# A recurrent-memory attention and a dilated local attention on one core: stage reports, output stores and a PSUM bank moved in the loop, working tiles and five weight units moved at its start

## The chip, the core and the metric

The kernel runs on one core of a Trainium2 chip. A core has a matrix engine (PE, with weight loads listed apart as PEld), a vector engine (DVE), a scalar engine (ACT), a general engine (POOL), an engine that only issues and synchronises (SP), and 16 DMA engines that all queues share. The metric is the device time of one execution in microseconds (us); the kernel is compared by the median of several runs.

## What is computed

The input `x` is 2048 rows of 640 numbers. Two branches are mixed by a gate per row:

```python
g = sigmoid((x * gate_w).sum(-1))
a = A_ref(x, mem0, Wq, Wk, Wv, Wo)      # branch A
b = B_ref(x, wqkv, wo)                  # branch B
return g * a + (1 - g) * b
```

Branch B is attention of 32 heads of width 20 over 8 earlier rows with a step of 2. Branch A is a recurrence over 64 segments of 32 rows. Its attention has 32 heads of width 192:

```python
for s in range(64):
    h = concat([mem, x[32*s:32*s+32]])         # 8 + 32 = 40 rows
    q, k, v = h @ Wq, h @ Wk, h @ Wv           # 640 -> 32 heads x 192
    p = softmax(masked(q @ k.T * 192**-0.5))
    o = (p @ v) @ Wo                           # 40 rows x 640
    mem = o[:8]
    outs.append(o[8:])
```

Each segment needs the memory that the one before left, so the segments run one after the other.

## The kernel before

The kernel has four parts in order of time. `part_b` computes branch B and writes its result, already weighted, to DRAM (`bsc_dram`), together with the transposed segments (`xh_dram`). `prepass` computes, for all segments at once, the projections of the eight last rows of each segment, and stores them to `zpk_dram`: first q and k (tiles `ZS`, pool `pre_zs`), then v (tiles `ZV`, pool `pre_zv`). `part_a` runs the recurrence. `part_z` finishes the eight last rows of every segment from `oz_dram`.

**Weights.** The weights of branch A do not all fit into SBUF. `weights_setup` splits them into units. Nine are loaded early, most of the others by `load_late(0)`, `load_late(1)` (in `prepass`, ahead of its v part) and `load_late(2)` (the last three units of `ob`, ahead of `part_a`). The 21 half units of the list `STREAM` are read from DRAM again in every segment, through a ring of seven slots (`wst`). `pump` issues the loads on SP's queue. A slot is loaded anew when PE has finished with the unit seven places back; the text numbers these units 0 to 20 in the order of `STREAM`.

**A segment.** `segment("head", ...)` projects q and k: `m_qk(0)` to `m_qk(3)` with units 0 to 5 of the stream, copies out of PSUM by `c_qk` on ACT, block transposes by `t_qk` on DVE. `segment("rest", ...)` does `m_qk(4)`, `m_qk(5)`, the scores in two halves, the softmax (`e_exp`, `e_sum`, `e_norm`), the v projection in three thirds (`m_v(0)` to `m_v(2)`, copied out by `c_v`), the product with the values (`pv_half`), and the output projection (`o_group`). At its end the memory rows go back into `hT` (`pick`), and the next head starts. `m_qk(i)` writes the PSUM banks `X[:,0]`, `X[:,1]`, `Ms[0]`, `Ms[1]`, `Ms[0]`, `X[:,1]` for i = 0 to 5.

**The loop.** The order of every engine's instructions in `part_a` is written out by hand (`manual_schedule`). The first segment and a head are unrolled; then `For_i` (line 1017) runs 62 passes, each a rest followed by the head of the next segment; a last rest follows. A pass is cut by `tc.stage_boundary()` into four stages: stage 0 from the start of the rest to `m_v(1,(0,))`, stage 1 to `o_group("oa", 3)`, stage 2 into the head behind `m_qk(0,(0,1,2))`, stage 3 to the end. Within a stage `done(engine)` (`tc.previous_stage_wait`) is a report of that engine: it waits until all that this engine issued in the previous stage, its DMAs included, has finished, and says so to the others. No engine enters the next stage before all five have reported in the present one; entering stage 0 of the next pass follows the same rule. Behind the entry, each engine resets semaphores and goes on. `held()` is SP's report followed by a halt of the pump until the next boundary. All these instructions carry line 1017 in the profile.

In a head of the loop the reports stand in this order: POOL, behind the two stores `store_z`; DVE behind `mix`; ACT behind `c_qk(1)`; SP and PE at the very end, behind `m_qk(3)`. SP's queue in the head holds the loads of units 6 to 12.

**Stores.** `store_z(s, h)` issues on POOL a DMA from `zst[h]` to `oz_dram[h]`. `zst[0]` is a part of `KW` (`aK` in the profile), which `c_qk(2)` of the next head overwrites; `zst[1]` is a part of `vz` (`aVz`), which `load_vz`, on POOL at the start of the rest, overwrites. In the loop both stores of segment s are issued in the next head, behind its stage boundary.

**The tiles of part A.** `part_a` allocates the working tiles (`aP`, `aK`, `aVz`, `aSel`, `aH`, `aG`), fills the selection masks (`build_sel`: small memsets on DVE, 40 or so selections on POOL), and loads the first segment into `aH`; then `load_z(0)` and `load_vz(0)` follow. All of it stands behind the release of the tiles of `prepass`.

Of the kernel before, what the change touches and what calls it, by code (L numbers as in the profile page):

```python
# [10 lines left out]
BF = mybir.dt.bfloat16  # L11
# [2 lines left out]

SLOTS = 7
N_EARLY = 9
LATE0 = 101376
STREAM = [("q", 0, 1, 1), ("k", 0, 1, 1), ("k", 0, 3, 1), ("q", 1, 1, 0), ("k", 1, 0, 0), ("k", 1, 3, 1), ("q", 2, 2,
          0), ("k", 2, 0, 1), ("k", 2, 1, 1), ("k", 2, 4, 1), ("v", 0, 3, 1), ("v", 1, 1, 0), ("v", 1, 4, 1), ("v", 2,
# [7 lines left out]
class _K:  # L27
# [381 lines left out]
    def weights_setup(self):  # L409
        nc, tc = self.nc, self.tc  # L410
        rest = [k for u in self.slice_keys() for k in self.parts(u) if k not in STREAM]
        first = ["q", "k", "v", "oa", "ob"]
        rest = sorted(rest, key=lambda k: first.index(k[0]))
        self.early, late = rest[:N_EARLY], rest[N_EARLY:]
        self.late = ([], [], late[-3:])
        used = 0
        for k in late[:-3]:
            used += 2 * self.width(k)
            self.late[int(used > LATE0)].append(k)
        self.wres = self.ctx.enter_context(tc.tile_pool(name="wres", bufs=1))  # L420
        self.res_tiles = {}
        self.wscr = {}
        self.wstream = self.ctx.enter_context(tc.tile_pool(name="wstream", bufs=1))
        self.slots = [self.wstream.tile([128, 1024], BF, name=f"wst{i}") for i in range(SLOTS)]
        self.slot_at, self.streaming = 0, False
# [77 lines left out]
    def prepass(self):  # L503

        nc, tc, KC = self.nc, self.tc, self.KC
        nseg = self.S // self.seg
        NZ = nseg * 8
        self.zpk_dram = self.dram.tile([nseg, 128, 1152], BF, name="zpk_dram")
        with tc.tile_pool(name="pre_zv", bufs=2, side="right", reuse_waits="tile") as zvp:
            zTi = zvp.tile([128, KC, NZ], BF, name="zTi", bufs=1)  # L510
            with tc.tile_pool(name="pre_zs", bufs=2, reuse_waits="tile") as zp, \
                    tc.tile_pool(name="pre_zt", bufs=1, reuse_waits="tile") as ztp:
                zT = ztp.tile([128, KC, NZ], BF, name="zT")
                nc.scalar.dma_start(zT[:], self.zT_dram[:].rearrange("p c s i -> p c (s i)"))
                nc.gpsimd.tensor_copy(zTi[:].rearrange("p c (i s) -> p c i s", i=8),
                                      zT[:].rearrange("p c (s i) -> p c i s", i=8))
                for m in ("q", "k"):
                    n = 16 if m == "q" else 24
                    for c in range(48):
                        if c % n == 0:  # L520
                            ZS = zp.tile([128, nseg, 192], BF, name="ZS")
                        if c % 16 == 0:
                            sls = [self.get_columns(m, c // 16, kc) for kc in range(KC)]
                        ps = self.pst([128, NZ], F32, name="ps_pre")
                        for kc in range(KC):
                            nc.tensor.matmul(ps[:], lhsT=sls[kc][c % 16],
                                             rhs=zT[:, kc, :], start=(kc == 0), stop=(kc == KC - 1))
                        zc = 8 * (c % 16) if m == "q" else 16 * (c % 12) + 8 * (c // 12 % 2)
                        self.evac(ZS[:, :, zc:zc + 8], ps[:].rearrange("p (s i) -> p s i", i=8))
                        if c % n == n - 1:  # L530
                            if m == "q":
                                zs = [(256 * (c // n) + 128, 0, 128)]
                            elif c < n:
                                zs = [(0, 0, 128), (256, 128, 64)]
                            else:
                                zs = [(320, 0, 64), (512, 64, 128)]
                            for z0, f, w in zs:
                                nc.scalar.dma_start(self.zpk_dram[:, :, z0:z0 + w].rearrange("s p f -> p s f"),
                                                    ZS[:, :, f:f + w])
            self.load_late(1)  # L540
            for t in range(3):
                sls = [self.v_columns(t, kc) for kc in range(KC)]
                for st in range(NZ // 128):
                    ZV = zvp.tile([128, 2048], BF, name="ZV")
                    pss = [self.pst([128, 512], F32, name="ps_pre") for _ in range(4)]
                    for kc in range(KC):
                        for j in range(4):
                            nc.tensor.matmul(pss[j][:], lhsT=zTi[:, kc, 128 * st:128 * st + 128],
                                             rhs=sls[kc][j], start=(kc == 0),
                                             stop=(kc == KC - 1))  # L550
                    for j in range(4):
                        self.evac(ZV[:, 512 * j:512 * j + 512], pss[j][:])
                    for k in range(2 * st, 2 * st + 2):
                        for e, R, x, n in self.V_PIECES[t]:
                            nc.scalar.dma_start(self.zpk_dram[:, 8 * R + k:128:32, 768 + x:768 + x + n],
                                                ZV[64 * (k % 2):64 * (k % 2) + 64, :].rearrange(
                                                    "s (j e) -> s j e", j=4)[:, :, e:e + n])

    def build_sel(self, W, ones):
        nc = self.nc  # L560
# [26 lines left out]
    def part_a(self):  # L587
# [2 lines left out]
        scale_a = float(self.Dh) ** (-0.5)  # L590
        ctx = ExitStack()
        with ctx:
            pers = ctx.enter_context(tc.tile_pool(name="a_pers", bufs=1))
            work = ctx.enter_context(tc.tile_pool(name="a_work", bufs=1))
            PP, KW, vz, sel, h_, a4 = (pers.tile([128, n], BF, name=x) for x, n in (
                ("aP", 2304), ("aK", 1024), ("aVz", 384), ("aSel", 188), ("aH", 160), ("aG", 162)))
            self.build_sel(sel, PP[:, 0:160])
            p0 = (128, 896, 1664)
            P = [PP[:, f:f + 640].rearrange("p (b c i) -> p b c i", b=5, i=8) for f in p0]
            Px = [PP[:, f + 128:f + 640] for f in p0]  # L600
# [33 lines left out]
            def row(t, s):  # L634
                return t[bass.ds(s, 1)].rearrange("o p f -> p (o f)")

            def load_seg(s, dst=xh):
                nc.sync.dma_start(dst, row(self.xh_dram, s))

            def load_z(s):  # L640
                nc.sync.dma_start(PP[:, 0:2304].rearrange("p (g f) -> p g f", g=3)[:, :, 0:256],
# [7 lines left out]

            def load_a4(s):  # L650
                nc.sync.dma_start(a4[:].bitcast(I32), self.bsc_dram[bass.ds(32 * s, 32)].rearrange("t j f -> j t f"))

            load_seg(0, h_[:])
            load_z(0)
            load_vz(0)

            def tail():
                pa = Ss[0][:, 0, :]
# [22 lines left out]
            def segment(part, prev, s, nxt, looped=False):  # L681
# [123 lines left out]

                def m_v(t, kcs=range(KC)):
                    if t not in pvs:
                        pvs[t] = Ms[1 - t % 2]
                    for kc in kcs:
                        sl = self.v_columns(t, kc)  # L810
                        burst([nc.tensor.matmul(pvs[t][32 * j:32 * j + 32, :], lhsT=hT[:, kc, :],  # L811
# [4 lines left out]

                def c_v(t):

                    (nc.vector.tensor_copy if t == 0 else nc.scalar.copy)(Px[t], pvs[t][:])  # L819

                def pv_half(h):
                    E = Es[h]
# [76 lines left out]
                if part == "head":  # L899
                    self.used = 0  # L900
                    m_qk(0, (0, 1, 2))
                    stage()
                    if prev is not None:
                        store_z(prev, 0)
                        store_z(prev, 1)
                    done(POOL)
                    m_qk(1, (0,))
                    if prev is not None:
                        pick("ob", Ss[1])
                    m_qk(1, (1, 2))  # L910
                    if prev is not None:
                        pa, ms = tail()
                        burst(ms)
                    m_qk(0, (3, 4)); m_qk(1, (3, 4))
                    if prev is not None:
                        mix(pa)
                    done(DVE)
                    c_qk(0); c_qk(1)
                    done(ACTE)
                    t_qk(0); t_qk(1)  # L920
                    m_qk(2, range(KC)); c_qk(2); t_qk(2)
                    m_qk(3, range(KC)); c_qk(3); t_qk(3)
                    done(SP)
                    done(PE)
                    return
                self.end = len(STREAM) if nxt is None else None
# [50 lines left out]
                for i2 in range(4):  # L977
                    o_group("oa", i2)
                stage()
                if nxt is None:  # L980
                    store_z(s, 0)
                done(POOL)
                pairs = pv_half(1)
                done(PE)
                c_o(1, pairs)
                c_z(1, pairs, 0); c_z(1, pairs, 1)
                done(ACTE)
                if nxt is None:
                    store_z(s, 1)
                if nxt is None:  # L990
                    self.sort_oz(0)
                for i2 in (4, 5):
# [17 lines left out]

            ctx.enter_context(tc.manual_schedule(engines=set(ALL)))
            self.start_stream()
            segment("head", None, 0, 1)
            segment("rest", None, 0, 1)
            self.sent -= len(STREAM)
# [69 lines left out]
def kernel(  # L1085
# [20 lines left out]
    with tc.tile_pool(name="psum", bufs=8, space=bass.MemoryType.PSUM) as k.psum:  # L1106
        with tc.issue_after(k.first_store):
            k.prepass()
    k.load_late(2)
    k.part_a()  # L1110

_INS = ['A_x', 'A_mem0', 'A_Wq', 'A_Wk', 'A_Wv', 'A_Wo', 'A_seg_len', 'B_x', 'B_wqkv', 'B_wo', 'gate_w']
# [29 lines left out]
```

## Time and profile before

| what | us |
|---|---|
| median of 3 runs (1679.66 to 1682.4) | 1680.38 |
| the profiled execution | 1679.99 |
| its span, first to last instruction | 1678.5 |
| branch B, to about | 229 |
| `prepass`, about | 229 to 428 |
| first matmul of `part_a` | 430 |
| one pass of the loop, mean (POOL's `load_vz`, 62 times from 462.6 to 1574.0) | 18.2 |
| `part_z` and the end, from about | 1606 |

The page of the profile gives the busy time of each engine. The waits view lists which engine waited for which, with the line of each: `PE psm L714 <- ACT aK L721` means that a matmul of line 714 writing PSUM tile `psm` waited for the ACT instruction of line 721 that writes `aK`. The timeline lists instructions in order, start and duration first; square brackets give the idle time of the engine before the instruction and what ended it. A "q" behind an engine's name is its sequencer: waiting, branching, issuing. The view of one source line gives counts, durations in ns (least, median, most), and the first and last start. The view of windows gives, for each stretch, its length, the busy time of PE, PEld, DVE, ACT and POOL, the granted clock of PE, the busy share of the DMA engines, and GB/s.

### The profile page before, as it was taken

What the parts mean: (1) busy time and instruction counts of PE and PEld (TensorE: products, weight loads), DVE (VectorE), ACT (ScalarE), POOL (GpSimd) and SP (SyncE); (2) the same over time, 40 slices, a digit from 0 to 9 for tenths busy, and PEclk for the clock granted to TensorE, in tenths of its full rate; (3) what the DMA queues carried; (4) which work ended last, traced back from release to release, by engine and by line L of the source; (5) the groups of instructions that cost most, each with busy time, mean ns of one, the idle gap of its engine ahead of it and who ended that gap; (6) DMA issues with size and microseconds to landing.
All of it is one profiled execution on the core that took longest, in us unless ns stands there. A gap on an engine that the chain in (4) does not pass through costs nothing. (4 is left out here: it accounts for less than half of the span.)

```text
span 1678.5 us, 91617 instructions
## 1 busy us (share of the span) xinstructions
PE 1486.7 (89%) x37462; PEld 852.0 (51%) x37477; DVE 802.7 (48%) x1936; ACT 656.1 (39%) x1609; POOL 143.2 (9%) x275
## 2 busy tenths in 40 slices
PE   6898897997689999999999999999999999999878
PEld 3455553343345555555555555555555555555457
DVE  4556542222345555555555555555555555555520
ACT  3766741212233433433433433443443343443340
POOL 4002000000200010010000001001001001001000
PEclk9999999999799999999999999999999999999989
DMA  6931059789679999999999999999999999999981
GB/s 165 215 101 53 31 157 266 181 204 290 213 247 317 307 316 318 301 305 320 307 300 318 314 301 311 314 306 317 315 303 312 316 305 310 317 310 310 316 209 28
DMA packets 438730, 438.32 MB, mean 261 GB/s; under 512 B 194172, under 2 KB 306820, under 8 KB 438660
## 3 DMA queue, kind: packets, MB, share of 16 engines
q1 hardware_dynamic: 344344, 395.02, 73.2%
q10 hardware_dynamic: 87148, 29.72, 7.2%
q0 software_dynamic: 7168, 12.60, 2.2%
q8 instruction: 51, 0.84, 0.2%
q14 instruction: 19, 0.16, 0.0%
HBM read 402.83 MB, written 39.48 MB: 264 GB/s over the span
## 5 line engine op out<-in xcount | busy, mean ns | idle before, releaser
L714 PEld LDWEIGHTS <-aH 128*32 128x32 bf16 x7680 | 201.2, 96 | 277.2 <-PE psm L714 79.6
L811 PE MATMUL psm<-wlate_v,aH 128*32 128x512 bf16 x3200 | 250.9, 382 | 18.1 <-DVE aP L819 16.7
L721 ACT CAST aP<-psx 128x512 bf16<-128x512 f32 x128 | 68.8, 589 | 327.9 <-PE psx L714 327.9
L714 PE MATMUL psx<-wlate_k,aH 128*32 128x512 bf16 x1920 | 195.6, 385 | 0.0
L874 PEld LDWEIGHTS <-aP 128*32 128x32 bf16 x6144 | 160.1, 96 | 64.1 <-ACT aP L853 23.1
L874 PE MATMUL psm<-wlate_oa,aP 128*32 128x384 bf16 x2560 | 167.7, 329 | 0.0
L714 PE MATMUL psm<-wlate_q,aH 128*32 128x512 bf16 x1408 | 108.8, 381 | 59.7 <-ACT aK L721 50.6
L734 DVE STREAM_TRANSPOSE aK<-aP 128x512 bf16<-128x512 bf16 (+1 forms) x256 | 142.6, 557 | 13.4 <-ACT aP L721 0.3
L714 PE MATMUL psx<-wst,aH 128*32 128x512 bf16 x768 | 138.8, 384 | 3.4 <-DMA wst<-wscr 3.4
L811 PEld LDWEIGHTS <-aH 128*32 128x32 bf16 x3840 | 94.5, 97 | 82.5 <-issue 20.0
L731 DVE STREAM_TRANSPOSE aP<-aP 128x512 bf16<-128x512 bf16 x128 | 91.1, 712 | 89.2 <-ACT aP L721 89.0
L874 PE MATMUL psm<-wst,aP 128*32 128x384 bf16 (+1 forms) x896 | 128.9, 306 | 4.7 <-DMA wst<-wscr 4.7
L874 PE MATMUL psm<-wlate_ob,aP 128*32 128x256 bf16 x2688 | 125.3, 273 | 0.4 <-issue 0.4
L811 PE MATMUL psm<-wst,aH 128*32 128x512 bf16 x640 | 124.7, 383 | 0.0
L714 PE MATMUL psx<-wres_q,aH 128*32 128x512 bf16 x1152 | 97.4, 385 | 19.1 <-DMA aH<-xh_dram 14.6
L853 DVE CAST aP<-psx 128x128 bf16<-128x128 f32 (+2 forms) x192 | 75.6, 422 | 70.5 <-PE psx L841 70.4
L773 ACT ACTIVATE aK<-psS 128x224 bf16<-128x224 f32 x128 | 46.1, 360 | 148.8 <-PE psS L765 148.8
L774 DVE TENSOR_TENSOR aK<-aK,aSel 128x224 bf16<-128x224 bf16 x128 | 35.3, 275 | 139.1 <-ACT aK L773 138.6
L714 PE MATMUL psm<-wst,aH 128*32 128x512 bf16 x512 | 99.6, 380 | 0.9 <-DMA wst<-wscr 0.6
L853 ACT CAST aP<-psS 128x384 bf16<-128x384 f32 (+2 forms) x192 | 65.4, 375 | 83.5 <-PE psx L841 81.6
L648 POOL DMA_DIRECT2D oz_dram<-aK x64 | 34.6, 541 | 734.8 <-DMA aVz<-zpk_dram 712.9
L819 ACT CAST aP<-psm 128x512 bf16<-128x512 f32 x128 | 75.4, 589 | 47.3 <-PE psS L765 45.0
(164 smaller groups left out, 2750.5 us busy)
## 6 DMA issues: line engine op xcount, KB each, us to landing
wst<-wscr SPq DMA_DIRECT2D x965, 256.0 KB, 4.4
wst<-wscr SPq DMA_DIRECT2D x384, 192.0 KB, 3.5
aP<-zpk_dram SPq DMA_DIRECT2D x64, 192.0 KB, 3.1
zpk_dram<-ZS ACTq DMA_DIRECT2D x5, 2048.0 KB
aVz<-zpk_dram POOLq DMA_DIRECT2D x64, 96.0 KB, 4.0
wlate_k<-in_A_Wk_dram SPq DMA_DIRECT2D x8, 512.0 KB
wres_q<-in_A_Wq_dram SPq DMA_DIRECT2D x7, 512.0 KB
wst<-in_A_Wk_dram SPq DMA_DIRECT2D x14, 256.0 KB
```

What stands on the lines that cost most here:

```text
L648: nc.gpsimd.dma_start(row(self.oz_dram[h], s), zst[h])
L714: burst([nc.tensor.matmul(pq[32 * j:32 * j + 32, :], lhsT=hT[:, kc, :], rhs=sl[j], start=(kc == 0), stop=(kc == KC - 1), tile_position=(0, ...
L721: nc.scalar.copy(st[i], pqs[i])
L731: nc.vector.transpose(P[p][:, 1:5, :, :].rearrange("p b c i -> p c b i"), st[i])
L734: nc.vector.transpose(KT[:, c0:c1, :].rearrange("p c k -> p (c k)"), st[i] if part is None else st5[part])
L773: nc.scalar.activation(E, pSs[h][:, :, 0:112], ACT.Exp, scale=scale_a)
L774: nc.vector.tensor_tensor(out=E, in0=E, in1=self.mask[h].unsqueeze(1).to_broadcast([128, 2, 112]), op=ALU.mult)
L811: burst([nc.tensor.matmul(pvs[t][32 * j:32 * j + 32, :], lhsT=hT[:, kc, :], rhs=sl[j], start=(kc == 0), stop=(kc == KC - 1), tile_position ...
L819: (nc.vector.tensor_copy if t == 0 else nc.scalar.copy)(Px[t], pvs[t][:])
L853: (nc.scalar.copy, nc.vector.tensor_copy)[g](x.rearrange("p (j c q) -> p j c q", j=2, q=32), pairs[g][:, :, 0:240].rearrange("p j (c q) -> ...
L874: ms.append(nc.tensor.matmul(pso[part][32 * jj:32 * jj + 32, 0:n], lhsT=oT_slot(R // 2, j, 3 * (R % 2) + t), rhs=self.o_weights(osl, part, ...
```

## The change

In the loop:

- `store_z(s, 0)` and `store_z(s, 1)` are issued in the rest of their own segment: the first right behind the boundary into stage 2, the second behind `c_z(1)` and ACT's report. The two stores in the head are gone, and POOL reports there right behind the boundary.
- In the head a one-column memset of `zst[0]` on DVE is added ahead of `mix`.
- ACT's report and SP's report stand behind `c_qk(2)`, ahead of `t_qk(2)` and `m_qk(3)`. PE's report stays at the end.
- `m_v(0)`, `m_v(1)`, `m_v(2)` write `X[:,0]`, `Ms[0]`, `Ms[1]` instead of `Ms[1]`, `Ms[0]`, `Ms[1]`.

At the start of part A:

- The working tiles are allocated and the masks built in `prepass`, between its q and k part and its v part, in the space that `pre_zs` and `pre_zt` left, with waits tile by tile. The first segment is loaded into `aH` behind `load_late(1)`.
- `load_late(1)` loads two units of `ob` fewer and `load_late(2)` five instead of three. `load_late(2)` is called inside `part_a` behind `start_stream` (seven stream loads), `load_z(0)` and `load_vz(0)`.

```diff
+N_LAST = 5
-        self.late = ([], [], late[-3:])
+        self.late = ([], [], late[-N_LAST:])
-        for k in late[:-3]:
+        for k in late[:-N_LAST]:
@@ prepass
+            self.working_tiles()
             self.load_late(1)
+            nc.sync.dma_start(self.work[4][:], self.xh_dram[0:1].rearrange('o p f -> p (o f)'))
             for t in range(3):
...
+    def working_tiles(self):
+        pers = self.ctx.enter_context(self.tc.tile_pool(name="a_pers", bufs=1, reuse_waits="tile"))
+        PP, KW, vz, sel, h_, a4 = self.work = [pers.tile([128, n], BF, name=x) for x, n in (
+            ("aP", 2304), ("aK", 1024), ("aVz", 384), ("aSel", 188), ("aH", 160), ("aG", 162))]
+        self.build_sel(sel, PP[:, 0:160])
@@ part_a
-            pers = ctx.enter_context(tc.tile_pool(name="a_pers", bufs=1))
...
-            self.build_sel(sel, PP[:, 0:160])
+            PP, KW, vz, sel, h_, a4 = self.work
...
-            load_seg(0, h_[:])
-            load_z(0)
-            load_vz(0)
...
-                        pvs[t] = Ms[1 - t % 2]
+                        pvs[t] = (X[:, 0], Ms[0][:], Ms[1][:])[t]
...
                     m_qk(0, (0, 1, 2))
-                    stage()
-                    if prev is not None:
-                        store_z(prev, 0)
-                        store_z(prev, 1)
-                    done(POOL)
+                    stage(POOL)
...
                     if prev is not None:
+                        nc.vector.memset(zst[0][:, 0:1], 0.0)
                         mix(pa)
                     done(DVE)
                     c_qk(0); c_qk(1)
-                    done(ACTE)
                     t_qk(0); t_qk(1)
-                    m_qk(2, range(KC)); c_qk(2); t_qk(2)
+                    m_qk(2, range(KC)); c_qk(2)
+                    done(ACTE, SP)
+                    t_qk(2)
                     m_qk(3, range(KC)); c_qk(3); t_qk(3)
-                    done(SP)
                     done(PE)
...
                 stage()
-                if nxt is None:
-                    store_z(s, 0)
+                store_z(s, 0)
                 done(POOL)
                 pairs = pv_half(1)
...
                 done(ACTE)
-                if nxt is None:
-                    store_z(s, 1)
+                store_z(s, 1)
...
             self.start_stream()
+            load_z(0)
+            load_vz(0)
+            self.load_late(2)
...
-    k.load_late(2)
     k.part_a()
```

## The prediction

> **What bounds the kernel now.** I read the page first, for the engine that is the bound; then windows, for where it is not; then the waits in the loop; then timeline and source lines of one pass, the one from 1007.5 to 1025.5, to see what ends the largest wait.
>
> The page's busy times:
>
> ```profile
> PE 1486.7 (89%) x37462; PEld 852.0 (51%) x37477; DVE 802.7 (48%) x1936; ACT 656.1 (39%) x1609; POOL 143.2 (9%) x275
> ```
>
> PE is the bound, and an edit is worth only the PE idle time that it ends. Windows: the start of part A, the loop, and two stretches of one pass.
>
> ```profile
> 416.00:430.00 14.00, 0.00 (x0) 0.00 (x0) 1.89 (x9) 1.07 (x2) 1.30 (x5) 0.62 0.79 230
> 430.00:475.00 45.00, 36.29 (x851) 18.01 (x855) 16.83 (x42) 13.78 (x35) 8.16 (x36) 0.84 0.64 209
> 475.00:1575.00 1100.00, 1008.14 (x30745) 586.83 (x30741) 581.06 (x1511) 438.65 (x1209) 98.72 (x183) 1.00 0.93 310
> 1008.00:1015.00 7.00, 6.13 (x144) 4.32 (x136) 3.29 (x6) 2.15 (x4) 1.56 (x3) 1.00 1.03 374
> 1018.00:1024.00 6.00, 5.53 (x242) 3.61 (x238) 3.41 (x13) 3.18 (x11) 0.00 (x0) 1.00 0.85 250
> ```
>
> In the loop PE lacks 92 of 1100 us, some 1.5 per pass. DMA is almost as full (0.93), and full in the head and early rest. PE stands still for 14 us at the start. The waits in the loop, then the turn from one pass to the next:
>
> ```profile
> PE psm L714 <- ACT aK L721: 50.6, 56, 1.8
> ```
>
> ```profile
> 1011.46 0.95 SPq L463 DMA_DIRECT2D wst<-wscr  x2
> 1011.75 0.48 PE L714 MATMUL psm<-wlate_k,aH 128*32 128x512 bf16 x4
> 1012.27 0.59 ACT L721 CAST aK<-psm 128x512 bf16<-128x512 f32 x1 [1.01 <-PE psm L714]
> ...
> 1013.09 0.40 PE L714 MATMUL psm<-wlate_q,aH 128*32 128x512 bf16 x4 [0.87 <-ACT aK L721]
> ```
>
> The idle 0.87 us ahead of `m_qk(4)` is put down to `c_qk(2)`, whose bank it overwrites. But that copy ended at 1012.86. The loop's own instructions at the same place:
>
> ```profile
> L1017 SPq EVENT_SEMAPHORE  x11: 17/17/28, 1012.5 to 1013.4; - x11
> ...
> L1017 ACTq EVENT_SEMAPHORE  x3: 17/17/17, 1010.2 to 1012.7; - x3
> L1017 DVEq EVENT_SEMAPHORE  x1: 21/21/21, 1009.4 to 1009.4; - x1
> ...
> L1017 PEldq COMPARE_BRANCH  x1: 208/208/208, 1011.6 to 1011.6; - x1
> ```
>
> DVE reported at 1009.4, ACT at 1010.2, PE at 1011.36, then branched (to 1011.82). SP's report (1012.45 to 1012.61) comes last: its queue holds the load of unit 12, issued about 1012.09. At 1012.63 the next record of every engine follows, and `m_qk(4)` starts 0.45 later. So the wait is the loop's entry held by SP, every pass alike: `m_qk(4)` starts 0.43 behind SP's report in nearly all 58 passes I followed, and 1.27 us on average behind the last matmul start of `m_qk(3)`, where PE's usual pace is 0.215.
>
> **Part 1, the reports.** SP's report moves ahead of `m_qk(3)` and its loads. It waits for the DMAs of the stage before, unit 5 last (landed 1011.30 here), so about 1011.5; ACT's, behind `c_qk(1)`, is at 1011.25 or so, and behind `c_qk(2)` in program order but ahead of its completion. POOL's waits for the landing of `store_z(1)`, below. PE is then the last: its branch ends 1011.82; PE itself shows no entry without a wait, so I bound it: 0.06 us (its first-pass branch not taken) to 0.53 (the smallest gap seen). I take 0.13, which other engines show between branch and next record, plus the same 0.45: `m_qk(4)` at 1012.40 instead of 1013.09, 0.69 saved here and 0.74 in the mean pass. ACT's later place (1010.2 to 1011.25) remains ahead of PE.
>
> The next bound takes a part of it. `held()` halts SP in `m_v(0)` until units 6 to 12 have landed; unit 12 lands 3.16 us behind `m_qk(4)` on average, and the boundary usually falls 3.5 behind it. One pass shows what happens if it is late:
>
> ```profile
> L1017 SPq EVENT_SEMAPHORE  x1: 655/655/655, 526.6 to 526.6; - x1
> ```
>
> ```profile
> 526.57 0.60 PE L811 MATMUL psm<-wlate_v,aH 128*32 128x512 bf16 x8
> 527.54 0.28 PE L789 MATMUL psS<-aK,aSel 128*32 128x160 bf16 x8 [0.37 <-DVE aK L734]
> ```
>
> There unit 12 landed at 527.22, and `e_sum` came 4.50 us behind `m_qk(4)` instead of the constant 3.96. With `m_qk(4)` earlier by 0.7 and the weights where they are, 3.16 + 0.7 = 3.86 passes 3.5 by 0.36; the mean landing is helped by part 2's move of stores. I take a loss of 0.2 per pass, bounds 0 and 0.45. Net 0.7 - 0.2 = 0.5 per pass, times 62 = **31 us**.
>
> **Part 2, the stores.** Two POOL issues per pass move from head to rest, 0.54 us each (the page's `POOL DMA_DIRECT2D oz_dram<-aK` row, 541 ns); POOL is 9% busy, so nothing by itself, and only POOL's report and `load_vz` are queued behind them. By their timing `store_z(0)` is issued about 3.3 us ahead of the head's first matmul, `store_z(1)` 1.9 ahead, landing 4.2 to 5.0 us later: POOL's report at 2.6 behind that matmul, against an entry at 4.1. That cover of 1.5 us is what a slow store would have to use up. `c_qk(2)`, which today starts 0.10 us behind the landing of `store_z(0)` (44.0 us in 35 waits), is no longer held by it. That wait is off the path, since the copy's end and not its start could hold `m_qk(4)`: it then ends near 1012.4 in place of 1012.86, the same time as the entry, cost nothing to 0.2 (in the bounds above). Its start is then set by its matmuls.
>
> The stores' transfers leave the full stretch (1008 to 1015), about 0.23 us of all 16 queues' time, and `load_vz`, behind `store_z(1)`, moves into it, 0.15 to 0.28. These cancel to within 0.1, below nothing or above. In the full stretch units 0 to 5 have a slack of only 0.04 to 0.3; waits on landings there cost 0.16 per pass now and I keep that.
>
> The memset on DVE is new: 60 ns, from the nearest short memset row. It must wait for `store_z(0)` to land, about 1008.8, with `mix` behind it at 1009.3 and the whole of DVE's queue behind that. Cost nothing: DVE idles 1.10 us ahead of its first transpose here. If the store landed 1.6 later, it would be in the path.
>
> **Part 3, V's bank.** It removes these PE waits of the loop:
>
> ```profile
> PE psm L811 <- DVE aP L819: 16.2, 59, 0.3
> ```
>
> 0.27 per pass, yet `pv_half(0)` behind it waits for `c_v(1)` on ACT (1000.73 to 1001.32 in the pass ahead; `pv_half` at 1001.37), whose start is set by the scores, not by `m_v`. PE would arrive earlier and wait longer. I take 0; bounds 0 and -0.27, in total 0 to -16.2 us.
>
> **Part 4, the start.** First the cause of the 14 us, then the wait of unit 7:
>
> ```profile
> PE psx L714 <- DMA aH<-xh_dram: 14.6, 1, 14.6
> PE psx L714 <- DMA wst<-wscr: 3.4, 1, 3.4
> ```
>
> `aH` would be there early, so PE starts near 421, behind the last copy of `prepass` (421.13), not 430.05. But the head needs unit 7 at some 428.5, and its load stands on SP's queue behind `load_z(0)` (which needs the `zpk_dram` stores, landed 427.8 now; up to 3 earlier without three `ob` loads beside them) and the five `ob` loads of 384 KB, about 1.27 us each: it lands at 434 to 438, against 440.63. So 9 us of idle go and most return as a wait for unit 7: gain 3 to 6, I take **4**. Against it: the selections and memsets of `build_sel` stand in `prepass` ahead of the copies of its v part, and wait there for the ZS stores, done about 366.5. That phase is bound by DMA, so I cost them at 0, up to +5 if that cover is gone. In the first pass PE's clock is low in either version (0.84 in the window 430 to 475), no difference.
>
> **Sum.** 1679.99 - 31 - 4 = 1645. The profiled execution is 1679.99 (span 1678.5, 1.5 around it), 0.39 under the median of 1680.38: no correction.
>
> **A rule to weigh.** The profile's DMA view of 600 to 1500 lists queues q1, q0 and q10 and none for instructions, 51 and 19 packets of those in the whole run; so PE's backward branch is not followed by a code load here.
> The Trainium skill, "Runtime: NRT & Kernel Launch", section Instruction fetch mechanics, says that a taken branch to code outside the two pages that an engine holds makes it wait for a DMA fetch of the target. The body of a pass is some 1,000 PE instructions, so by that rule PE would be late at the entry, and the sum would be that of case C below; the trace, which shows no such fetch in the loop, speaks against it.
>
> **Rivals.**
> *B, both gates vanish*: stage 1's boundary costs nothing, because the head's loads come earlier with PE; 62 x 0.74 = 46, start 6: 1628; with a part of V's 0.27 as well, about 1620. For: DMA has room over a pass (0.85 at 1018 to 1024). Against: 3.86 against 3.5 above.
> *C, half the gain*: PE's entry takes 0.53 behind the branch, or unit 12 takes the 0.45. 0.74 - 0.45 = 0.3, times 62 = 18.6, start 3: 1658. For: PE's branch takes 208 ns where those of ACT and SP take 45.
> *D, slower*: `m_v(0)` now writes `X[:,0]` while `c_qk(5)` still copies out of `X[:,1]`. Should the wait be by the whole tile, `m_v(0)` stands until that copy ends.
>
> ```profile
> 1015.75 1.03 PE L811 MATMUL psm<-wlate_v,aH 128*32 128x512 bf16 x14
> ```
>
> ```profile
> L725 ACT CAST aP<-psx x1: 372/372/372, 1017.2 to 1017.2; 128x256 bf16<-128x256 f32 x1
> ```
>
> From 1015.75 to 1017.16 + 0.37 = 1017.53 and a semaphore is 1.85 us; less 0.7, +1.15 a pass, 62 times = +71: 1679.99 + 71 - 4 = 1747. It decides as soon as the wait for `X` goes by tile. Against: `m_qk(5)` into one bank goes on while the other is read.
> *E, no gain*: `load_vz` and the stores of the next segment delay units 0 to 5, whose slack is 0.04 to 0.3, by 0.28, and units 6 to 12 by as much: 0.5 - 0.56 = about 0 a pass to +0.2; 1676 to 1688.
>
> **Numbers.** A (as summed) 0.45, own range 1634 to 1655; B 0.20; C 0.20; D 0.07; E 0.08, of which 0.03 lies within 0.2% (3.4 us, about what a measurement of this kernel can tell from no change) and 0.05 above. Faster 0.45 + 0.20 + 0.20 = 0.85, same 0.03, slower 0.12. The range takes A, C up to 1672 (C with its full bounds) and B down to 1622, and leaves D, E and B's end out.
>
> **What would show it.** Right: `m_qk(4)` some 0.5 us behind PE's branch, SP's report ahead of PE's; the row of 50.6 us falling to under 15; SP waiting in `m_v(0)` in many passes, and a new wait ahead of `e_sum`; the V wait gone and that of `pv_half` grown alike; PE's first matmul of part A near 421 and a wait for `wst` of 5 to 9 us. Wrong: SP or POOL still last at the entry (a store landing late), `m_v(0)` waiting for ACT's line 725, waits for `wst` in `m_qk(0)` to `m_qk(3)` grown, or a longer `prepass`.

## The result: 4.3% slower

| | us |
|---|---|
| kernel before, median of 4 runs (1679.66 to 1687.71) | 1681.39 |
| changed kernel, median of 4 runs (1753.11 to 1755.64) | 1754.57 |
| ratio, with its 95% interval | 1.0428 (1.0398 to 1.0457) |
| forecast | 1645, range 1622 to 1672 |

The forecast was wrong in sign. Its slower rival, D, had 1747 and a chance of 0.07.

In the changed kernel's profile the lines that carry this are the busy times of the page, the window of the loop, and PE's waits in the loop, in this order. The numbers of the code lines have moved: `m_qk` is L716, `c_qk` L723 to L727, `e_sum` L791, `m_v` L813, `o_group` L876, the loop is still L1017.

```profile
PE 1510.5 (86%) x37462; PEld 864.0 (49%) x37477; DVE 809.4 (46%) x1999; ACT 667.5 (38%) x1609; POOL 143.1 (8%) x275
```

```profile
475.00:1575.00 1100.00, 965.59 (x28802) 560.31 (x28792) 551.23 (x1473) 421.24 (x1131) 92.07 (x170) 1.00 0.88 291
```

```profile
PE psx L813 <- ACT aP L727: 94.1, 57, 1.7
PE psS L837 <- ACT aP L821: 8.6, 56, 0.2
PE psm L716 <- PE psm L716: 5.1, 21, 0.4
PE psx L716 <- DMA wst<-wscr: 2.3, 9, 0.4
```

PE's busy share of the loop fell (from 1008 to 966 of 1100 us) and so did DMA's (0.93 to 0.88): both wait for something else. The 50.6 us ahead of `m_qk(4)` are gone, as forecast. In their place stands a wait of 1.65 us in every pass: the first matmul of the v projection waits for `c_qk(5)`'s second copy. The timeline of one pass shows it:

```profile
1007.22 0.61 PE L716 MATMUL psx<-wlate_k,aH 128*32 128x512 bf16 x6
1007.45 0.38 PE L716 MATMUL psx<-wst,aH 128*32 128x512 bf16 x2
...
1008.17 0.39 ACT L725 CAST aP<-psx 128x256 bf16<-128x256 f32 x1
...
1009.07 0.37 ACT L727 CAST aP<-psx 128x256 bf16<-128x256 f32 x1 [0.50 <-DVE aP L733]
1009.49 0.83 PE L813 MATMUL psx<-wlate_v,aH 128*32 128x512 bf16 x12 [1.65 <-ACT aP L727]
```

`m_qk(5)` ends at 1007.8; the copy ends at 1009.44; `m_v(0)` starts 0.05 later. The copy reads `X[:,1]`, `m_v(0)` writes `X[:,0]`.

The turn of the loop, on the other hand, went as intended. The loop's own instructions around one turn of the changed kernel:

```profile
L1017 SPq EVENT_SEMAPHORE  x5: 17/27/28, 1004.0 to 1005.4; - x5
L1017 PEldq EVENT_SEMAPHORE  x4: 51/51/51, 1004.0 to 1005.1; - x4
L1017 ACTq EVENT_SEMAPHORE  x3: 17/17/17, 1003.8 to 1005.1; - x3
...
L1017 PEldq COMPARE_BRANCH  x1: 208/208/208, 1004.3 to 1004.3; - x1
```

POOL reported at 1003.33, ACT at 1003.84, PE at 1004.08, SP at 1004.15; PE's branch ended at 1004.53, its next record is at 1004.59, and `m_qk(4)` starts at 1005.00. SP's report stands 0.34 us or more ahead of the end of PE's branch in every turn but the first and the last. So PE's own branch, and no report, sets the entry.

Where the time went, as means over the passes, in us (starts of the first matmul of each, and of the last one of `m_qk(3)`, which is meant below where `m_qk(3)` is said to end; the first two columns count from the head's first matmul, the next four from `m_qk(4)`, and the pass is from one head to the next). The experiments of the next section are added, to be read with it:

| kernel | last of `m_qk(3)` | `m_qk(4)` | `m_v(0)` | `e_sum(0)` | `m_v(2)` | next head | pass |
|---|---|---|---|---|---|---|---|
| before | 4.41 | 5.68 | 2.66 | 3.97 | 5.75 | 12.45 | 18.13 |
| changed | 4.64 | 5.17 | 4.49 | 5.78 | 7.24 | 14.18 | 19.35 |
| e1 old V banks | 4.68 | 5.23 | 2.67 | 4.35 | 5.89 | 12.78 | 18.01 |
| e2 V banks alone | 4.50 | 5.97 | 4.49 | 5.78 | 7.24 | 14.18 | 20.15 |
| e3 `m_qk(5)` in Ms[1] | 4.70 | 5.21 | 2.67 | 4.33 | 5.79 | 12.73 | 17.94 |
| e4 reports alone | 4.47 | 5.55 | 2.67 | 3.97 | 5.75 | 12.47 | 18.02 |
| e5 second store back | 4.44 | 4.93 | 2.67 | 4.18 | 5.64 | 12.69 | 17.62 |
| e6 boundary 1 later | 4.63 | 5.16 | 2.67 | 4.41 | 5.65 | 12.69 | 17.84 |
| e7 boundary 2 earlier | 4.39 | 4.90 | 2.66 | 4.42 | 5.88 | 13.22 | 18.12 |
| e11 second store by ACT | 4.64 | 5.19 | 2.67 | 4.32 | 5.77 | 12.73 | 17.91 |
| e9 entry 2 freed | 4.43 | 4.97 | 2.68 | 4.20 | 5.65 | 12.64 | 17.61 |

Per pass: `m_qk(4)` 0.51 earlier, the rest of the pass 1.73 longer, together +1.22, times 62 = +76 us. The start gave 3 back (the second head begins at 451.75 in place of 454.85): 73, as the profiled executions differ (1753.11 against 1679.99).

### The profile page after: what moved, and what is told of

It reads as the page before. It is cut to its first block, busy times and chain, and to the rows that moved or that the text cites. A ratio compares the mean times of both kernels' runs of the same rounds, so it can differ in the third digit from the quotient of the medians.

```text
span 1751.6 us, 91542 instructions
## 1 busy us (share of the span) xinstructions
PE 1510.5 (86%) x37462; PEld 864.0 (49%) x37477; DVE 809.4 (46%) x1999; ACT 667.5 (38%) x1609; POOL 143.1 (8%) x275
## 5 line engine op out<-in xcount | busy, mean ns | idle before, releaser
L716 PEld LDWEIGHTS <-aH 128*32 128x32 bf16 x7680 | 206.7, 96 | 235.0 <-issue 51.8
L716 PE MATMUL psx<-wlate_k,aH 128*32 128x512 bf16 x1920 | 201.8, 385 | 0.0
L723 ACT CAST aP<-psx 128x512 bf16<-128x512 f32 x128 | 68.8, 589 | 333.9 <-PE psx L716 329.6
L876 PEld LDWEIGHTS <-aP 128*32 128x32 bf16 x6144 | 162.4, 96 | 59.0 <-ACT aP L855 18.1
L813 PEld LDWEIGHTS <-aH 128*32 128x32 bf16 x3840 | 94.8, 97 | 177.6 <-issue 126.8
L813 PE MATMUL psm<-wlate_v,aH 128*32 128x512 bf16 x2048 | 180.5, 381 | 0.0
L813 PE MATMUL psx<-wlate_v,aH 128*32 128x512 bf16 x1152 | 81.9, 384 | 105.1 <-ACT aP L727 105.1
L876 PE MATMUL psm<-wlate_oa,aP 128*32 128x384 bf16 x2560 | 166.9, 327 | 0.0
L716 PE MATMUL psx<-wst,aH 128*32 128x512 bf16 x768 | 139.2, 384 | 9.3 <-DMA wst<-wscr 8.3
L876 PE MATMUL psm<-wst,aP 128*32 128x384 bf16 (+1 forms) x896 | 128.5, 305 | 5.8 <-DMA wst<-wscr 5.8
L876 PE MATMUL psm<-wlate_ob,aP 128*32 128x256 bf16 x2688 | 125.2, 273 | 1.7 <-issue 1.7
L716 PE MATMUL psm<-wlate_q,aH 128*32 128x512 bf16 x1408 | 111.6, 382 | 13.1 <-PE psm L716 5.3
L716 PE MATMUL psx<-wres_q,aH 128*32 128x512 bf16 x1152 | 104.6, 387 | 10.1 <-ACT ZV L74 5.7
L813 PE MATMUL psm<-wst,aH 128*32 128x512 bf16 x512 | 100.6, 383 | 0.6 <-issue 0.6
L716 PE MATMUL psm<-wst,aH 128*32 128x512 bf16 x512 | 99.8, 380 | 0.7 <-DMA wst<-wscr 0.4
```

The costliest lines, as they stand in the source:

```text
L716: burst([nc.tensor.matmul(pq[32 * j:32 * j + 32, :], lhsT=hT[:, kc, :], rhs=sl[j], start=(kc == 0), stop=(kc == KC - 1), tile_position=(0, ...
L723: nc.scalar.copy(st[i], pqs[i])
L876: ms.append(nc.tensor.matmul(pso[part][32 * jj:32 * jj + 32, 0:n], lhsT=oT_slot(R // 2, j, 3 * (R % 2) + t), rhs=self.o_weights(osl, part, ...
```

## Experiments

Each ratio is against the kernel before on the same chip, where its median was 1685; 95% intervals in brackets. e1 to e4 and e5 to e8 each ran side by side.

### e1 and e2: the V banks taken back, and the V banks alone

e1 is the changed kernel with one line undone; e2 is the kernel before with only the opposite edit.

```diff
-                        pvs[t] = (X[:, 0], Ms[0][:], Ms[1][:])[t]
+                        pvs[t] = Ms[1 - t % 2][:]
```

> The changed kernel with the v projection in its old PSUM banks (Ms[1], Ms[0], Ms[1]); all else as changed. Theory T (the wait of m_v(0) for the second copy of c_qk(5) is the whole slowdown): the interval from m_qk(4) to the next head's first matmul, 14.18 us in the changed kernel, returns to 12.45, or up to 0.2 more if stage 1's entry now holds; with m_qk(4) 0.5 us earlier in the pass that gives 0.3 to 0.5 us a pass, 19 to 32 us, and about 3 us at the start: 1646 to 1658. Rival R1 (DMA is the bound once the period is short: the waits on units 0 to 5, which grew by 0.23 us a pass even in the slow version, grow further): 1665 to 1680. Rival R2 (the bank is not the cause, but what moved ahead of m_v(0), say ACT's later copies): stays near 1750.

> The kernel before with the v projection in the new banks and nothing else changed. T: m_v(0) at 1015.75 would stand until the copy's end at 1017.53 and a semaphore, +1.75 to 1.85 us a pass, 62 to 64 times: 1788 to 1797. R2 (the slowdown needs the other parts too): 1680, or a little below by V's old wait of 0.27 us a pass, 1664 to 1680.

Measured: e1 0.989 (0.986 to 0.992), 1666.4 us. e2 1.074 (1.071 to 1.077), 1811 us. PE's first waits in e2's loop (475 to 1560), where the lines have their old numbers (L811 is `m_v`, L725 the second copy):

```profile
PE psx L811 <- ACT aP L725: 88.8, 54, 1.7
PE psm L714 <- ACT aK L721: 58.7, 53, 1.8
```

With the other parts gone and this edit alone, the wait for the copy is there in full, beside the old one at the loop's turn. In e1 it is gone and `m_v(0)` is back at 2.67. The V banks are the whole slowdown, and rival R2 falls. e2 is 126 us slower on 1685, 9 to 18 more than expected: its pass is 20.15, which is 18.13 + 1.73, and another 0.29 ahead of `m_qk(4)`. There the first store has a part: `m_qk(4)` starts 0.05 us behind the end of `c_qk(2)` in 40 of 61 passes (21 of 61 in the kernel before), and `c_qk(2)` starts 0.10 us behind the landing of that store in all of them. Why the landing is later in e2 was not followed. e1 lies above its theory's numbers (0.989 is 1663 on 1681), at the edge of R1's: the turn, from the end of `m_qk(3)` to `m_qk(4)`, gained 0.72 (1.27 before, 0.55 in e1), but `m_qk(3)` ends 0.27 later, and `e_sum(0)` 0.38.

### e3: the same banks, and `c_qk(5)` out of X

```diff
-            pqs = [Ms[i % 2] if i // 2 == 1 or i == 4 else X[:, i % 2] for i in range(6)]
+            pqs = [Ms[i % 2] if i // 2 == 1 or i >= 4 else X[:, i % 2] for i in range(6)]
```

> The changed kernel with m_qk(5) writing Ms[1] in place of X[:,1], so that c_qk(5) no longer reads any part of X when m_v(0) writes X[:,0]. The two regions never overlapped. T (the wait goes by the tile X, not by its banks): the wait for line 727 disappears, time as in the run with the old V banks or a little less, since V's old wait of 0.27 us a pass is gone too: 1640 to 1658. Rival (a true conflict on X[:,0], for instance by scores or by the copies' order on ACT): stays near 1750.

Measured: 0.991 (0.987 to 0.995), 1666.9 us. PE's first waits in its loop (475 to 1560):

```profile
PE psS L791 <- DVE aK L736: 12.1, 23, 1.0
PE psS L837 <- ACT aP L821: 10.5, 65, 0.2
PE psm L716 <- PE psm L716: 4.4, 18, 0.4
```

`m_v(0)` still writes `X[:,0]` and no longer waits, only because nothing reads the other half of `X` any more. The wait goes by the tile `X`: the program orders the instructions of two engines on one tile, though they touch different banks. The Trainium skill, "PSUM — Partial Sum Buffer", section PSUM bank collisions raise a hardware error, has accesses by two engines to different banks run clean, and asks for a guard by bank and quadrant; by that rule the wait was not needed. No run here lets the two run side by side, so the trace shows only that the wait is the program's and that another bank assignment is rid of it. The old V wait, 16.2 us in the loop before, is only 3.0 us in 13 waits in e1 with the old banks, and the times of e1 and e3 are the same within their intervals: V's bank without the conflict shows no gain that these runs can tell.

### e4: the reports alone

The kernel before with the reports of ACT and SP behind `c_qk(2)`; stores and banks as before.

```diff
-                    done(ACTE)
                     t_qk(0); t_qk(1)
-                    m_qk(2, range(KC)); c_qk(2); t_qk(2)
+                    m_qk(2, range(KC)); c_qk(2)
+                    done(ACTE, SP)
+                    t_qk(2)
                     m_qk(3, range(KC)); c_qk(3); t_qk(3)
-                    done(SP)
                     done(PE)
```

> The kernel before with SP's and ACT's reports behind c_qk(2), stores and V's banks as before. c_qk(2) then still waits for the landing of store_z(0) (1012.17 in the pass read), and ACT's report stands behind it in ACT's queue: the loop's entry moves from 1012.63 to some 1012.3 at best, m_qk(4) 0 to 0.3 us earlier. T2 (the reports need the moved stores to be worth anything): 1662 to 1680. Rival (the reports alone carry the gain of 0.5 us a pass): 1645 to 1655.

Measured: 0.995 (0.993 to 0.997), 1678.5 us. `m_qk(4)` starts 0.13 us earlier in the pass, and the row that the change was to end stays, as the first of PE's waits in the loop (475 to 1560):

```profile
PE psm L714 <- ACT aK L721: 42.1, 59, 1.6
```

Here the row is to be taken at its word. In 60 of 61 passes `c_qk(2)` starts 0.10 us behind the landing of the first store, and `m_qk(4)`, which writes the bank that this copy reads, starts 0.05 us behind the copy's end; the report that moved ahead is no longer what it waits for. So the reports are worth little while `c_qk(2)` waits for the first store: they need the moved store, as expected, though it is the copy itself, and not ACT's report behind it, that holds PE. (The stores moved, with the reports left at their old places, was not tried, so whether the store needs the reports is open.)

### e5, e10 and e11: where the moved stores hurt

e5, e6, e7 and e11 are e3 with one thing changed. In e5 the second store is back in the head; e10 is e5 again, beside e9; in e11 the store stays in the rest, issued on ACT's queue.

```diff
@@ e5, e10
-                    stage(POOL)
+                    stage()
+                    if prev is not None:
+                        store_z(prev, 1)
+                    done(POOL)
...
-                store_z(s, 1)
+                if nxt is None:
+                    store_z(s, 1)
@@ e11
-                nc.gpsimd.dma_start(row(self.oz_dram[h], s), zst[h])
+                (nc.gpsimd, nc.scalar)[h].dma_start(row(self.oz_dram[h], s), zst[h])
```

> The third run's kernel (m_qk(5) in Ms[1]) with the second store, store_z(s, 1), back in the next head behind its stage boundary; the first store and the reports stay moved. In the third run the last matmul of m_qk(3) starts 4.70 us behind the head's first, 4.41 before the change. T3 (the moved stores' transfers lie beside the loads of units 0 to 5 and make them late): the interval falls by about half of the growth, to 4.50 to 4.60, and the time by 6 to 12 us, unless units 6 to 12 become as much later. Rival (units 0 to 5 are late because the pass is shorter, whatever the stores do): stays 4.65 to 4.75, time the same or slower.

> The fifth run's kernel again, beside the ninth on the same chip: ratio 0.978 within 0.006 if the first measurement stands.

> The third run's kernel with the moved second store, store_z(s, 1), issued on ACT's queue in place of POOL's, at the same place in the rest. The third run's loads of units 3 to 5 land 4.97 to 5.36 us behind their issue, the fifth's (store back in the head) 4.54 to 4.94, while that store keeps the 16 DMA engines busy for only some 0.12 us. T6 (it is POOL's queue that holds the loads up): the loads land in 4.5 to 5.0, m_qk(3)'s last matmul returns to 4.4 to 4.5, the time to 1646 to 1652. Rival (it is the time of the store, whatever its queue): 4.65 to 4.75, and 1664 to 1670. A store on ACT's queue also waits for ACT's earlier work and lands behind ACT's report; if that becomes the loop's entry, the gap before m_qk(4) grows from 0.19.

Measured: e5 0.978 (0.972 to 0.984), 1646 us; e10 0.978 (0.975 to 0.980), 1647 us; e11 0.985 (0.982 to 0.989), 1662 us. The loads of units 3, 4 and 5 land (median, behind their issue):

| | unit 3 | unit 4 | unit 5 |
|---|---|---|---|
| before | 4.58 | 4.85 | 5.02 |
| e3 | 4.97 | 5.16 | 5.36 |
| e5 | 4.54 | 4.76 | 4.94 |
| e11 | 4.88 | 5.13 | 5.31 |
| e7 (below) | 4.62 | 4.84 | 5.02 |

With the second store back in the head all of the delay is gone, not half: `m_qk(3)` ends at 4.44, and the pass is 0.32 shorter than in e3, 20 us in all. The windows of the loop before, in e3 and in e5:

```profile
475.00:1560.00 1085.00, 995.26 (x30347) 579.50 (x30343) 573.41 (x1490) 432.73 (x1193) 97.46 (x180) 1.00 0.93 310
```

```profile
475.00:1560.00 1085.00, 1026.95 (x30712) 587.02 (x30707) 581.72 (x1572) 447.07 (x1207) 98.37 (x182) 1.00 0.94 314
```

```profile
475.00:1560.00 1085.00, 1038.36 (x31192) 593.42 (x31188) 591.88 (x1597) 455.88 (x1230) 99.63 (x184) 1.00 0.96 319
```

DMA moves more per us in e5 than in e3, so its total was not e3's limit (R1 as stated falls for that kernel); moving the second store took the delay away. Its queue is not the cause: on ACT's queue the loads are as late (4.88 to 5.31) and `m_qk(3)` ends at 4.64. e11's ratio is below e3's, but their intervals overlap. Why a transfer that takes the 16 engines 0.12 us makes three loads 0.4 us late is not settled. The store's place alone does not make them late: in e7 it is where it is in e3, issued 1.64 us ahead of the head's first matmul, but the loads of units 0 and 1 are issued 0.40 us further ahead of that matmul, and units 3 to 5 land as early as before the change.

### e6: the boundary into stage 1 later

```diff
-                m_v(1, (0,))
+                m_v(1, (0, 1))
                 stage(POOL)
...
-                m_v(1, (1, 2, 3, 4))
+                m_v(1, (2, 3, 4))
```

> The third run's kernel with the boundary into stage 1 (and e_sum(0) behind it) one group of four v matmuls later, 0.2 us. T4 (the entry of stage 1 waits for the landing of units 6 to 12, and 0.28 us a pass are lost there: 12.73 against 12.45 from m_qk(4) to the next head): the interval falls by 0.1 to 0.2, the time by 6 to 12 us against the third run. Rival (the loss is in the softmax chain behind e_sum, which now starts later): the interval grows by up to 0.2, 12 us slower than the third run.

Measured: 0.987 (0.981 to 0.992), 1661.6 us, against e3's 0.991 (0.987 to 0.995): inconclusive. The interval from `m_qk(4)` to the next head fell by only 0.04. PE does what it did behind the boundary before it, and `scores(1)` starts 0.14 earlier, but half of that is lost ahead of `pv_half(1)` (1.06 us behind the first `o_group`, 0.99 in e3), which now waits for ACT's copy in `c_z` too (30 times, 7.6 us; no such wait in e3).

### e7 and e9: the boundary into stage 2 earlier

```diff
@@ e7 (on e3) and e9 (on e5)
-                for i2 in range(4):
+                for i2 in range(2):
                     o_group("oa", i2)
                 stage()
                 store_z(s, 0)
                 done(POOL)
+                for i2 in range(2, 4):
+                    o_group("oa", i2)
                 pairs = pv_half(1)
@@ e9 only
                     load_z(nxt)
-                    load_a4(s)
...
                 m_v(2, (2,))
                 held()
+                if nxt is not None:
+                    load_a4(s)
```

> The third run's kernel with the boundary into stage 2 two groups of the output projection earlier, behind o_group(oa, 1). The loads of units 0 and 1 wait for that boundary 1.24 and 0.74 us after their slots are free, while the DMA engines fall to some 7.5 of 16 busy, 2.75 us ahead of the head. T3 (units 0 to 5 are late, so DMA's order and not its total is the limit): the loads start some 0.4 us sooner, the interval to the last matmul of m_qk(3) falls from 4.70 to 4.4 to 4.5, the time by 12 to 18 us against the third run. Rival R1 (the DMA engines are busy 0.94 of the loop, their total is the limit): what the head gains, stage 1's entry loses, less than 5 us. Another: the entry of stage 2 waits for SP's report there and PE stands, slower.

> The fifth run's kernel (m_qk(5) in Ms[1], second store back in the head) with the boundary into stage 2 behind o_group(oa, 1), as in the seventh, and load_a4 issued behind SP's report of stage 1 and not ahead of it. In the seventh run SP's last report stood behind load_seg, load_z, load_a4 (0.6 us each on SP's queue) and a weight load, and PE waited 0.40 us a pass for it. T5 (that queue, and not DMA's total, made the seventh run slow): the report comes some 0.6 us sooner, the interval from the first o_group to pv_half(1) returns from 1.39 to 1.0, units 0 and 1 are loaded earlier, and the pass is 17.3 to 17.5 against 17.62 in the fifth run: 7 to 20 us faster than it, ratio 0.966 to 0.974. Rival R1 (DMA's total, busy 0.96 of the loop in the fifth run, is the limit): the pass stays 17.6.

Measured: e7 0.994 (0.991 to 0.997), 1675 us. `m_qk(3)` ends at 4.39, without the store being moved, but not because units 0 and 1 came sooner: SP issues the load of unit 0 on average 9.27 us behind `m_qk(4)`, 9.19 in e3. The head itself comes 0.49 later, and so the loads are ready for it. The last of the rivals came true: PE stands at the entry of stage 2 for SP's report. PE's and SP's timeline of one pass of e7 show it:

```profile
1014.20 0.51 PE L876 MATMUL psm<-wlate_oa,aP 128*32 128x384 bf16 x8
1015.16 0.50 PE L876 MATMUL psm<-wlate_oa,aP 128*32 128x384 bf16 x6 [0.44 <-DVE aK L804]
```

```profile
1012.39 0.34 SPq L644 DMA_DIRECT2D aK<-xh_dram  x1
1012.95 0.40 SPq L647 DMA_DIRECT2D aP<-zpk_dram  x1
1013.55 0.60 SPq L657 DMA_DIRECT2D aG<-bsc_dram  x1
1014.25 0.41 SPq L464 DMA_DIRECT2D wst<-wscr  x1
```

Four issues in a row, 0.6 us apart, and SP's report behind them at 1014.87; all engines enter at 1014.89. The 0.44 us of PE are put down to DVE, which merely goes on at the same entry. In e9, with one issue moved behind the report, that wait is gone: from the first `o_group` to `pv_half(1)` 1.00 us, 1.39 in e7. e9 gives 0.974 (0.972 to 0.976), 1642 us, the lowest ratio here (its interval touches e10's), and faster than both kernels of this case. But its pass is 17.61, e10's 17.59: what e9 has over e10, 0.974 against 0.978, is not in the pass of the profiled executions. The expected 17.3 to 17.5 did not come. R1 had 17.6, and DMA is busy 0.95 to 0.96 of the loop in both, but e9 does not decide for it, because its loads did not start sooner either: SP issues unit 0's 9.12 us behind `m_qk(4)`, 9.03 in e5. The issue that moved behind the report (0.59 us, `load_a4`) now stands in SP's queue ahead of that load, which follows it by 0.55 us in every pass. What loads that do start sooner would bring is open.

### e8: the start alone

The kernel before with all of the change's start part (working tiles in `prepass`, `N_LAST = 5`, the loads behind `start_stream`) and nothing of the loop.

> The kernel before with the start part of the change alone (working tiles in prepass, five ob units last). As predicted: PE starts part A some 9 us earlier, waits 5 to 9 us for unit 7, and the whole is 3 to 6 us shorter: ratio 0.9965 to 0.998. Rival: the masks hold up the v part of prepass and it is 0 to 5 us longer.

Measured: 0.996 (0.993 to 0.999), 6.6 us on 1685. PE's waits at the start, whole run of e8:

```profile
PE psx L716 <- ACT ZV L74: 5.2, 1, 5.2
PE psx L716 <- DMA wst<-wscr: 5.2, 1, 5.2
```

The wait of 14.6 us for `aH` has become 5.2 us for the last copy of `prepass` and 5.2 for unit 7.

## Why the prediction was wrong, step by step

- **Part 3, V's bank: the step that failed.** It was costed at 0, with bounds of 0 and -0.27 us a pass: the removed wait was weighed, the added one was not in the sum. It stood among the rivals, with its price (+1.85 a pass; measured: `m_v(0)` 1.83 later, 1.73 at the next head). D's +1.15 a pass came out as +1.22: the turn's net gain was 0.51 and not 0.7, and the wait cost 1.73 and not 1.85. The reason given against D was no evidence: it named `m_qk(5)` writing one bank while the other is read, but at that time nothing reads `X[:,0]`. No row of the trace before had two engines on the two halves of `X` at once, and one row on record spoke for a wait by tile. Its lines, from the waits and the timeline of the kernel before:

```profile
ACT aP L721 <- PE psx L714: 304.8, 61, 5.2
```

```profile
1009.02 0.61 PE L714 MATMUL psx<-wres_q,aH 128*32 128x512 bf16 x6
1009.59 0.48 PE L714 MATMUL psx<-wlate_k,aH 128*32 128x512 bf16 x4
1010.18 1.07 ACT L721 CAST aP<-psx 128x512 bf16<-128x512 f32 x2 [4.99 <-PE psx L714]
```

The copy at 1010.18 is `c_qk(0)`, which reads `X[:,0]` alone. The last matmuls of `m_qk(0)`, which wrote that half, end at 1009.63; those of `m_qk(1)`, which write `X[:,1]`, end at 1010.07. In each of 57 passes followed the copy starts 0.12 to 0.13 us behind the end of `m_qk(1)` and at least 0.55 behind that of `m_qk(0)`. Where the banks are tiles of their own it is not so: in the changed kernel `c_qk(2)`, out of `Ms[0]`, starts 0.17 to 0.19 us behind `m_qk(2)`, while `m_qk(3)` still writes `Ms[1]`. So 0.07 went against a row that could be read at the time.
- **Part 1, the entry of the loop.** Right in the saving: from the end of `m_qk(3)` to `m_qk(4)` the mean fell from 1.27 to 0.53, 0.74 as forecast, and PE's next record is 0.06 us behind its branch (0.13 assumed). Case C's late entry did not come in the loop; only at the last turn, where the branch is not taken and PE leaves the loop, does `m_qk(4)` start 2.06 us behind it (0.47 in the median turn), and no run says why. But "every pass alike" read too much into the trace: SP's report ended under 0.47 us ahead of `m_qk(4)` in 37 of 61 passes, and in 21 of 61 `m_qk(4)` started 0.05 behind the end of `c_qk(2)`, mostly some 0.1 later than SP's report alone would have had it, so there the row that named the copy was right. The first store's wait was therefore not off the path, as part 2 has it; e4 shows it as the next bound. It did no harm to the sum, because that store moved too. The changed kernel's DMA view of 600 to 1500, too, lists no queue for instructions.
The rule of the Trainium skill, "Runtime: NRT & Kernel Launch", section Instruction fetch mechanics, would have a taken branch out of the two pages held wait for a fetch; the trace, with 0.06 us behind the branch, does not show one for PE.
- **Part 1, stage 1's entry.** Named rightly, sized low: 0.2 forecast, within 0 to 0.45; `e_sum(0)` is 0.38 later in e1 and 0.36 in e3, and 0.21 in e5. In e3 it is late in 49 of 61 passes, each time 0.29 us behind SP's report.
- **Part 2, the stores.** The issues on POOL, the memset and `c_qk(2)` cost nothing, and ACT's wait for the first store (44.0 us) is gone. But "these cancel to within 0.1" was wrong: the second store lands among the loads of units 0 to 5, whose slack of 0.04 to 0.3 the forecast itself had read, and costs 0.23 (changed kernel) to 0.29 (e3) us in the head. This is case E's mechanism: its 0.28 for the head came nearly in full; a price for units 6 to 12 is in the point above.
- **Part 4, the start.** Right. PE begins part A at 423.04 (421 forecast), waits 4.88 us for unit 7 and goes on at 435.56 (a landing at 434 to 438 was forecast); worth 6.6 us in e8, interval 2 to 11, against 4.

Without the V banks, the forecast of 1645 compares with e1 and e3: 0.989 and 0.991 of 1681 are 1663 and 1666, 18 to 21 us above. The head's 0.27 to 0.29 us a pass make 17 to 18 of it, and stage 1's entry, 0.28 to 0.33 at the next head against 0.2, another 5 to 8; the start gave back some 3. e5, with the store back, has the size of the forecast gain, 0.51 us a pass, but it is another kernel, with one store fewer moved and one more bank changed.

## What to carry to other kernels

When an edit changes the buffer that an instruction writes, list who touches any part of the same tile at that time: a wait can be by tile where the data are apart. An absent row does not speak against it; a reader that starts only when the writer of the tile's other half has ended speaks for it. In a pipeline full of DMA, a small transfer is priced by what lands behind it and how little slack that has, not by its own bytes. A report that gates every engine belongs ahead of the issues in its queue that it need not wait for, and what is put behind it then delays the loads that follow (e9); the wait that it causes can be put down to an engine that only goes on at the same entry.

## What was unexpected of the hardware

With a store that takes the 16 DMA engines some 0.12 us beside them, three weight loads in flight landed 0.4 us later (units 3 to 5: 4.54 to 4.94 us without, 4.97 to 5.36 with it), on POOL's queue and nearly as much on ACT's; with units 0 and 1 issued 0.40 us further ahead of the head (e7) they did not. And DMA, busy 0.93 of the loop before at 310 GB/s, reached 0.96 and 319 GB/s once the waits were gone.
